# Before the MoE: other weights in a planner's choice of engines, batch 0's subtractions off GpSimd, its squares on TensorE, loads on SyncE alone

## The chip, the cores and the metric

The program runs on one core of one Trainium2 chip. A core has five engines with one in-order instruction queue each: PE (TensorE, matrix multiplies), DVE (VectorE), ACT (ScalarE), POOL (GpSimd) and SP (SyncE, which here only issues DMAs), beside 16 DMA engines. Engines wait for each other through semaphores. The metric is the device time of one execution in microseconds (us).

## The reference

Block-sparse attention, and after it a two-layer network on all tokens. Cut to what is computed:

```python
# q, k, v: (4 batches, 8 heads, 768 tokens, 64); sampled_blocks: (24, 3)
scores = (1 / sqrt(64)) * q @ k.T
mask = |block_i - block_j| <= 1, or block_i or block_j is the first or the last, or block_j is sampled for block_i   # blocks of 32
scores = where(mask, scores, -1e9)
attn = exp(scores - max(scores)); attn = attn / (sum(attn) + 1e-9)
x = (attn @ v) as 3072 tokens x 512
h = x @ w_in                                   # 512 x 2048
g = maximum(h, 0) + alpha * minimum(h, 0)
out = g @ w_out                                # 2048 x 512
```

Everything is float32 in memory.

## The kernel before

**Numbers.** A float32 operand is scaled by a power of two and split into two float16 parts: hi is the rounded value and lo the rest. A product is three float16 matmuls (hi*hi, hi*lo, lo*hi). `times` makes hi (one instruction: L385 on ACT, L387 on DVE, L389 on POOL). `rest` makes lo: one instruction on DVE (L393), two on POOL (L395 scales, L396 subtracts hi). The scale comes from a norm: ACT squares the tile and sums along a row (`squares`, L381), PE sums over the rows (`tot`, L471), and DVE turns the total into a power of two (`pow2`, L373 and L376).

**The weights** come as 16 tiles `wi` and 16 tiles `wo` of 512 KB. Their raw words lie in slots while three steps repack them: `emit_n1` (DVE, L840), `emit_n2` (ACT L845 or DVE L847), `emit_n3` (DVE, L852). Then a Gram matrix on PE (L861) and its row maxima on DVE (L867) give the norm; hi and lo follow, lo of `wi` and of the first half of `wo` through PE (`d`, L937 and L938) and an ACT copy (L942), lo of the second half of `wo` on DVE or POOL. Only when all 32 tiles have a scale is the factor `gsc` there, without which no MoE work starts.

**Attention.** The 3072 tokens are 12 chunks of 256, three to a batch. A chunk has 4 head pairs ("units"), a unit 4 steps of 128 query rows and one head; 192 steps in all. A step is: scores `sp` on PE (two steps at once, L586 and L592), bias and row minimum `e` on DVE (L602), exp on ACT (L609), the reciprocal of the row sum on DVE (`dn` L614, `rs` L615), P hi and P lo (`ph`), and a transposing DMA `pt` that SP issues (L630). Unit by unit PE multiplies P with v (`av`, L665); ACT and DVE split the result into `x` (L676, L681).

**MoE.** Eight times per chunk: `emit_up` on PE (`h`, L1034), `emit_act` on DVE (`g`, L1044 and L1045), `gh` on ACT (L1050), `gl` on POOL (L1055) and `emit_down` on PE (`o`, L1076). The MoE of a chunk is laid beside the attention of the next ones.

**What sets the order.** Nothing of it is written out by hand. Every piece of work is an operation of a planner (`Plan`) with a priority, costs for each engine that may do it, the operations it needs and the buffers it takes. `Plan.run` steps through a model of the engines: of the ready operations, in order of priority, each goes to the engine with the least waiting plus weight (`PREF`) times cost. The resulting list is the program's order on every engine, and it is kept: each queue runs in that order, whatever the chip does. `MAX4` are the costs of hi, `LOW4` those of lo, `LQ` those of issuing a load. `PL` gives by step whether P lo goes to POOL (g) or DVE (v); `LD`, and buffer counts in `BUFS`, limit how far weight loads run ahead; `V_WA` to `W_WB` are priorities of the weights against the attention steps.

Of the kernel before, what the change touches and what calls it, by code (L numbers as in the profile page):

```python
# [217 lines left out]
def attn_moe(ctx: ExitStack, tc: tile.TileContext, q, k, v, sampled, w_in, w_out, alpha, out):  # L218
# [391 lines left out]

    def emit_rs(n):
        T["rs", n] = new_small("rs")
        dn = new_small("dn")
        nc.vector.tensor_scalar(dn, T["su", n], 1e-9, 1.0 / PSCALE, ALU.add, ALU.mult)  # L614
# [8 lines left out]

    def emit_p_t(n):
        u, j = steps[n]
        w = chunks[units[u][0]][2]
        h, i = divmod(j, w)
        if ("pt", u, h) not in T:
            T["pt", u, h] = wt("pt", [P, 2 * NT, w * P], F16)
        nc.sync.dma_start_transpose(  # L630
            T["pt", u, h][:, :, i * P : (i + 1) * P], T["ph", n].rearrange("p a s -> p (a s)")
        )

    def emit_p_pe(n, x):
        u, j = steps[n]
        w = chunks[units[u][0]][2]
        h, i = divmod(j, w)
        if ("pt", u, h) not in T:
            T["pt", u, h] = wt("pt", [P, 2 * NT, w * P], F16)
        t = T["tp", n, x] = ps_o.tile([P, 2 * DM], F16, tag="o", name="tp")  # L640
        for g in range(NT):
            nc.tensor.transpose(t[:, g * P : (g + 1) * P], T["ph", n][:, x, g * P : (g + 1) * P], ident16)

    def emit_p_copy(e, n, x):
        u, j = steps[n]
        w = chunks[units[u][0]][2]
        h, i = divmod(j, w)
        dst = T["pt", u, h][:, x * NT : (x + 1) * NT, i * P : (i + 1) * P]
        src = T["tp", n, x][:, :S].rearrange("p (x j) -> p x j", j=P)
        if e == "ACT":  # L650
            nc.scalar.copy(dst, src)
        else:
            nc.vector.tensor_copy(dst, src)
# [103 lines left out]
    def attend(n):  # L757
# [18 lines left out]
        if n < P_PE:
            o_pt[n] = []
            for x, src in ((0, o_hi), (1, o)):
                tb = plan.buf("o")
                t = plan.op(n - 2, {"PE": 0.4}, lambda x=x: emit_p_pe(n, x), [src], [tb, ptbuf[u, h]], [pb])  # L780
                o_pt[n].append(plan.op(n - 2, {"ACT": 0.85, "DVE": 0.9}, lambda e, x=x: emit_p_copy(e, n, x), [t], [ptbuf[u, h]], [tb]))
            return
# [442 lines left out]
```

## Time and profile before

| what | value |
|---|---|
| runs | 838.78, 841.10 and 843.01 us, median 841.1 |
| the profiled execution: its own time, its span | 840.87 us, 839.1 us |
| PE, DVE, ACT, POOL busy | 94%, 77%, 60%, 65% of the span |
| mean granted TensorE clock | 0.981 |
| first `up` matmul of the MoE | 134.9 us |

The profile is one execution. "Busy" of PE is modelled, since matmuls are pipelined. The view by windows gives busy time per engine in each stretch; the view by line groups equal instructions with their mean; the chain of waits is followed back from the last instruction; each row of a timeline is a start, a duration and an instruction. A duration on DVE or POOL contains what the instruction was held up after it had been started.

### The profile page before, as it was taken

What the parts mean: (1) busy time and instruction counts of PE and PEld (TensorE: products, weight loads), DVE (VectorE), ACT (ScalarE), POOL (GpSimd) and SP (SyncE); (2) the same over time, 40 slices, a digit from 0 to 9 for tenths busy, and PEclk for the clock granted to TensorE, in tenths of its full rate; (3) what the DMA queues carried; (4) which work ended last, traced back from release to release, by engine and by line L of the source; (5) the groups of instructions that cost most, each with busy time, mean ns of one, the idle gap of its engine ahead of it and who ended that gap; (6) DMA issues with size and microseconds to landing.
All of it is one profiled execution on the core that took longest, in us unless ns stands there. A gap on an engine that the chain in (4) does not pass through costs nothing.

```text
span 839.1 us, 16792 instructions
## 1 busy us (share of the span) xinstructions
PE 787.2 (94%) x6255; PEld 497.9 (59%) x6255; DVE 648.7 (77%) x1403; ACT 506.6 (60%) x868; POOL 549.3 (65%) x442
## 2 busy tenths in 40 slices
PE   4767759999999999999999999999999999999997
PEld 2324326566666666666666666566656666666664
DVE  6889999979977679788788778788787787676222
ACT  7888778766747457756556467766474575454111
POOL 8556556967777577677766768558685777566221
PEclk9989988999999999999999999999999999999999
DMA  9999697979997788898989699978997688667100
GB/s 320 299 241 237 139 213 132 201 150 172 197 181 158 132 153 164 184 173 152 201 167 176 117 164 198 168 148 179 189 188 136 134 159 141 120 114 108 46 12 26
DMA packets 386449, 136.13 MB, mean 162 GB/s; under 512 B 350628, under 2 KB 379328, under 8 KB 386368
## 3 DMA queue, kind: packets, MB, share of 16 engines
q1 hardware_dynamic: 372704, 118.66, 75.5%
q10 hardware_dynamic: 13600, 16.39, 6.8%
q8 instruction: 49, 0.80, 0.4%
q14 instruction: 32, 0.26, 0.1%
q0 software_dynamic: 64, 0.02, 0.0%
HBM read 35.67 MB, written 6.29 MB: 50 GB/s over the span
## 4 chain that ended last, share of the span: by engine, by line
PE 79%; DVE 11%; issue 4%; DMA 3%; ACT 2%; POOL 2%; POOLq 0%; DVEq 0%; ACTq 0%
PE o L1076 28%; PE h L1034 27%; PE av L665 11%; PE sp L586 6%; PE sp L592 4%; DVE e L602 3%; DVE ph L393 2%; PE d L937 1%; DVE wo L852 1%; DVE wi L840 1%; DMA kf<-in_k_dram 1%; DMA pt<-ph 1%; DMA raw<-in_moe_w_out_dram 1%; POOL v L389 1%; DVE wi L852 1%
## 5 line engine op out<-in xcount | busy, mean ns | idle before, releaser
L1034 PE MATMUL h<-x,wi 128*128 128x256 f16 x2304 | 267.2, 273 | 0.0
L1034 PEld LDWEIGHTS <-wi 128*128 128x128 f16 x2304 | 220.5, 98 | 48.0 <-issue 15.2
L609 ACT ACTIVATE e<-e,nm 128x768 f32<-128x768 f32 x192 | 178.5, 930 | 92.1 <-DVE nm L602 85.7
L1076 PE MATMUL o<-wo,gh 128*128 128x512 f16 x768 | 229.1, 380 | 0.0
L602 DVE CUSTOM_DVE_ANT_0 e<-sp,bias,cs 128x768 f32<-128x768 f32 x192 | 188.3, 1011 | 21.3 <-PE sp L592 21.1
L396 POOL TENSOR_TENSOR ph<-e,ph 128x768 f16<-128x768 f32 x96 | 179.3, 1868 | 8.0
L1055 POOL TENSOR_TENSOR gl<-g,gh 128x512 f16<-128x512 f32 x96 | 119.3, 1245 | 99.3 <-ACT gh L1050 83.0
L1050 ACT CAST gh<-g 128x512 f16<-128x512 f32 x96 | 59.0, 616 | 152.3 <-DVE g L1045 149.4
L1076 PE MATMUL o<-wo,gl 128*128 128x512 f16 x384 | 145.5, 379 | 0.6 <-POOL gl L1055 0.6
L389 POOL TENSOR_SCALAR ph<-e,rs 128x768 f16<-128x768 f32 x70 | 76.5, 1094 | 104.1 <-ACT e L609 63.3
L393 DVE SCALAR_TENSOR_TENSOR ph<-e,rs,ph 128x768 f16<-128x768 f32 x96 | 123.5, 1288 | 6.8 <-ACT ph L385 4.0
L1044 DVE SCALAR_TENSOR_TENSOR g<-h,am 128x512 f32<-128x512 f32 x96 | 65.9, 687 | 77.0 <-PE h L1034 76.3
L385 ACT ACTIVATE ph<-e,rs 128x768 f16<-128x768 f32 x117 | 108.2, 930 | 24.1 <-ACT e L609 7.7
L1076 PEld LDWEIGHTS <-gh 128*128 128x128 f16 x768 | 69.1, 98 | 86.6 <-issue 15.9
L395 POOL TENSOR_SCALAR e<-e,rs 128x768 f32<-128x768 f32 x96 | 95.8, 998 | 34.4 <-ACT ph L385 30.5
L665 PE MATMUL av<-pt,v 128*64 128x256 f16 x1728 | 109.5, 283 | 6.7 <-DVE nm L602 6.3
L665 PEld LDWEIGHTS <-v 128*64 128x64 f16 x1728 | 95.2, 113 | 23.1 <-issue 15.2
L1045 DVE SCALAR_TENSOR_TENSOR g<-h,gsc,g 128x512 f32<-128x512 f32 x96 | 72.1, 751 | 3.4
L1076 PEld LDWEIGHTS <-gl 128*128 128x128 f16 x384 | 37.5, 98 | 46.3 <-POOL gl L1055 1.1
L586 PEld LDWEIGHTS <-qt 128*128 128x128 f16 x384 | 37.2, 99 | 46.2 <-issue 13.8
L586 PE MATMUL sp<-kt,qt 128*128 128x512 f16 x192 | 47.8, 331 | 8.3 <-DVE nm L602 7.8
L586 PE MATMUL sp<-ks,qt 128*128 128x512 f16 x192 | 47.9, 332 | 7.5 <-DVE nm L602 7.5
(144 smaller groups left out, 762.0 us busy)
## 6 DMA issues: line engine op xcount, KB each, us to landing
wo<-in_moe_w_in_dram SPq DMA_DIRECT2D x13, 512.0 KB, 8.2
ks<-kt SPq DMA_DIRECT2D x30, 192.0 KB, 3.6
raw<-in_moe_w_out_dram SPq DMA_DIRECT2D x11, 512.0 KB, 6.7
qf<-in_q_dram SPq DMA_DIRECT2D x7, 512.0 KB, 5.2
out_dram<-ob ACTq DMA_DIRECT2D x14, 256.0 KB, 3.8
vf<-in_v_dram SPq DMA_DIRECT2D x9, 384.0 KB, 6.4
kf<-in_k_dram SPq DMA_DIRECT2D x8, 384.0 KB, 4.2
kf<-in_k_dram ACTq DMA_DIRECT2D x8, 384.0 KB, 4.7
```

What stands on the lines that cost most here:

```text
L385: nc.scalar.activation(dst, src, AF.Copy, scale=scale)
L389: nc.gpsimd.tensor_scalar(dst, src, scale, 1.0, ALU.mult, ALU.mult)
L393: nc.vector.scalar_tensor_tensor(dst, src, scale, hi, ALU.mult, ALU.subtract)
L395: nc.gpsimd.tensor_scalar(tmp, src, scale, 1.0, ALU.mult, ALU.mult)
L396: nc.gpsimd.tensor_tensor(dst, tmp, hi, ALU.subtract)
L586: nc.tensor.matmul(T["sp", n + i][:, a:z], T["qt", u][:, h, i, :], (ks, kt)[i][:, h, a:z], start=True, stop=False)
L602: nc.vector.tensor_tensor_reduce(T["e", n], T["sp", n], bias[:, t0 + j % w, :], scale=T["cs", c][:, hp : hp + 1], scalar=3.0e38, op0=ALU.a ...
L609: nc.scalar.activation(T["e", n], T["e", n], AF.Exp, bias=T["nm", n], scale=-1.0, accum_out=T["su", n])
L665: nc.tensor.matmul(av[h * D : (h + 1) * D, : n * P], v2[:, h, t, vv, :], T["pt", u, h][:, pl * NT + t, :], start=(m == 0), stop=(m == len( ...
L1034: nc.tensor.matmul(ph[:, i, :], win(w, f, ct), x[:, ct, :], start=(m == 0), stop=(m == len(terms) - 1))
L1055: nc.gpsimd.tensor_tensor(T["gl", c, j], T["g", c, j], T["gh", c, j], ALU.subtract)
L1076: nc.tensor.matmul(T["o", c][t], g[:, i, t * P : (t + 1) * P], wout(w, f), start=(i == 0 and m == 0 and j in first_j), stop=(i == 1 and m ...
```

## The change

- The numbers that set priorities and weights differ, and until 130 us of the planner's clock (140 before) a second set `PREF0` holds. `SLOW`, a surcharge on POOL's and some of DVE's costs in that time, falls from 1.25 to 1.12.
- For the first 22 steps P lo goes by `PL0` ("ggv": two of three to POOL); before every second one did. A step from 22 on goes by `PL` as before.
- Batch 0: lo of k and v is DVE's alone (`LOW0`); lo of the second half of `wo` is DVE's alone as well.
- Batch 0: the norms of k and v come from Gram matrices on PE (6 matmuls a tile, 48 in all) and row maxima on DVE, not from ACT's squares.
- `dn` is an operation of its own that ACT may do.
- Loads and stores are issued by SP alone (`LQ` without ACT); 42 of them stood in ACT's queue.
- Six weight loads may be under way (4 before). The pools `wr` (2 raw slots) and `g` (4) become one pool `wr` of 4, which raw `wo` tiles, `g` and the output tiles share.
- Code that no step used (a transpose of P on PE) is gone.

```diff
-MOE_LAG = 10.618
+MOE_LAG = 10.973
-MOE_BOOST = 1.211
-V_WA = -18.766
-W_WA = 0.754
-V_WB = 1.134
-W_WB = 0.607
-LDP = 30.529
-PL_V = -33.326
-P_V = 0.73
+MOE_BOOST = 1.244
+V_WA = -11.421
+W_WA = 0.818
+V_WB = 2.562
+W_WB = 0.788
+LDP = 47.514
+PL_V = -45.149
+P_V = 2.094
 PL = "gv"
-LD = 4
-P_PE = 0
+NS0 = 22
+PL0 = "ggv"
+LD = 6
-PREF = {"PE": 1.0, "DVE": 1.896, "ACT": 1.009, "POOL": 0.778, "SP": 1.0}
-SLOW = 1.25
-UNTIL = 140.0
+PREF = {"PE": 1.0, "DVE": 1.928, "ACT": 1.347, "POOL": 1.033, "SP": 1.0}
+PREF0 = {"PE": 1.0, "DVE": 2.5, "ACT": 1.0, "POOL": 0.8, "SP": 1.0}
+SLOW = 1.12
+UNTIL = 130.0
-BUFS = {"wr": 2, ... "x": 2, "g": 4, ...}
+BUFS = {"wr": 4, ... "x": 2, ...}
...
+                    pref = PREF0 if now < UNTIL else PREF
+                    best = min(o.alts, key=lambda e: max(idle[e] - now, hold(o, e)) + load[e] + pref[e] * cost(o, e))
...
-    LQ = {"SP": 0.47, "ACT": 0.5}
-    MAX4 = {"DVE": (0.55, 0), "ACT": 0.85, "POOL": 1.08}
+    LQ = {"SP": 0.47}
+    MAX4 = {"DVE": (0.55, 0), "ACT": 0.88, "POOL": 0.95}
     LOW4 = {"DVE": (0.94, 0), "POOL": (1.1, 1.7)}
+    LOW0 = {"DVE": (0.94, 0)}
...
+    def emit_gram_kv(key, start, stop):
+        if start:
+            T["gkv", key[0]] = ps_h.tile([P, 512], F32, tag="h", name="gkv")
+        top = T[key].rearrange("p h e -> p (h e)").bitcast(BF16).rearrange("p (e w) -> p e w", w=2)[:, :, 1]
+        for i in range(NT):
+            m = top[:, i * P : (i + 1) * P]
+            nc.tensor.matmul(T["gkv", key[0]][:, :P], m, m, start=start and i == 0, stop=stop and i == NT - 1)
+
+    def emit_gram_kv_max(key, acc):
+        nc.vector.tensor_reduce(acc, T["gkv", key][:, :P], AX.X, ALU.max)
...
+    def emit_dn(e, n):
+        T["dn", n] = new_small("dn")
+        if e == "ACT":
+            nc.scalar.activation(T["dn", n], T["su", n], AF.Identity, bias=eps, scale=1.0 / PSCALE)
+        else:
+            nc.vector.tensor_scalar(T["dn", n], T["su", n], 1e-9, 1.0 / PSCALE, ALU.add, ALU.mult)
...
-        o = plan.op(prio, {"ACT": 0.85}, lambda: emit_k_sq(b, hp), [o], [], [fb])
+        if b == 0:
+            gb = plan.buf("h")
+            o = plan.op(prio, {"PE": 0.9}, lambda: emit_gram_kv(("kf", b, hp), True, True), [o], [gb], [fb])
+            o = plan.op(prio, {"DVE": 0.28}, lambda: emit_k_gmax(b, hp), [o], [], [gb])
+        else:
+            o = plan.op(prio, {"ACT": 0.85}, lambda: emit_k_sq(b, hp), [o], [], [fb])
...
-        o = plan.op(prio, LOW4, lambda e: emit_k_lo(e, b, hp), [o], [], [nb, fb])
+        o = plan.op(prio, LOW0 if b == 0 else LOW4, lambda e: emit_k_lo(e, b, hp), [o], [], [nb, fb])
...
-        o = plan.op(n - 2, {"DVE": 0.3}, lambda: emit_rs(n), [o])
+        o = plan.op(n - 2, {"DVE": 0.15, "ACT": 0.26}, lambda e: emit_dn(e, n), [o])
+        o = plan.op(n - 2, {"DVE": 0.15}, lambda: emit_rs(n), [o])
+        path = PL0[n % len(PL0)] if n < NS0 else PL[n % len(PL)]
...
-            o_wo[y] = plan.op(p - 3 + 0.1 * (y % HF), {"DVE": (0.67, 0), "POOL": (0.8, 1.25)}, lambda e, y=y: emit_w_lo(e, "wo", y), [o])
+            o_wo[y] = plan.op(p - 3 + 0.1 * (y % HF), {"DVE": (0.67, 0)}, lambda e, y=y: emit_w_lo(e, "wo", y), [o])
```

The order on the engines follows from all of this together. On POOL, behind the set-up of the masks and identities, stood hi and lo of three of batch 0's four k tiles (`kn`; L395 and L396 are the two halves of a lo), with the scaled identities `sid` and hi of weights (`wi`) between them:

```order
L389 TENSOR_SCALAR kn<-kf,ks 128x12x64
L395 TENSOR_SCALAR kf<-kf,ks 128x768
L396 TENSOR_TENSOR kn<-kf,kn 128x12x64
L926 TENSOR_SCALAR sid<-ident,ssc 128x128
L389 TENSOR_SCALAR wi<-wi,ssc 128x512
L395 TENSOR_SCALAR kf<-kf,ks 128x768
L396 TENSOR_TENSOR kn<-kf,kn 128x12x64
```

At the same place, in the changed program:

```order
L944 TENSOR_SCALAR sid<-ident,ssc 128x128
L394 TENSOR_SCALAR wi<-wi,ssc 128x512
L944 TENSOR_SCALAR sid<-ident,ssc 128x128
L394 TENSOR_SCALAR kn<-kf,ks 128x12x64
L394 TENSOR_SCALAR wi<-wi,ssc 128x512
L394 TENSOR_SCALAR kn<-kf,ks 128x12x64 x3
L944 TENSOR_SCALAR sid<-ident,ssc 128x128
L394 TENSOR_SCALAR wi<-wi,ssc 128x512 x2
```

The subtractions are gone, all four hi of k are there, and hi of weights is met more often.

On SP, the first loads before (`wo` is the place where raw `w_in` tiles wait, `raw` a slot for `w_out`; loads of `qf` and further `kf` stood in ACT's queue):

```order
L419 DMA kf<-in_k_dram 128x2x384
L419 DMA wo<-in_moe_w_in_dram 128x4x256 x3
L419 DMA kf<-in_k_dram 128x2x384
L419 DMA raw<-in_moe_w_out_dram 128x1024 x2
L419 DMA wo<-in_moe_w_in_dram 128x4x256
```

and now:

```order
L425 DMA wo<-in_moe_w_in_dram 128x4x256 x4
L425 DMA raw<-in_moe_w_out_dram 128x1024 x2
L425 DMA kf<-in_k_dram 128x2x384
L425 DMA qf<-in_q_dram 128x8x128
L425 DMA kf<-in_k_dram 128x2x384
L425 DMA raw<-in_moe_w_out_dram 128x1024
```

Six weight tiles stand ahead of the first k tile, and all of it is one queue.

On DVE, the stretch that ends with the fourth `x` (the last input of the first `up`), before:

```order
L887 TENSOR_TENSOR am_116<-al,gsc 128x16
L373 TENSOR_SCALAR uq<-ssq 128x1
L376 TENSOR_SCALAR sq<-uq 128x1
L1060 TENSOR_SCALAR fs_1458<-sv,s_wi 128x1
L1061 TENSOR_SCALAR fs_1458<-fs_1458,s_wo 128x1
L1062 RECIPROCAL fs<-fs_1458 128x1
L393 SCALAR_TENSOR_TENSOR wo<-wo,swo 128x512
L681 SCALAR_TENSOR_TENSOR x<-av,x 128x256
```

and now, with the rows behind it:

```order
L905 TENSOR_TENSOR am_118<-al,gsc 128x16
L398 SCALAR_TENSOR_TENSOR wo<-wo,swo 128x512
L690 SCALAR_TENSOR_TENSOR x<-av,x 128x256
L645 RECIPROCAL rs<-dn 128x1 x2
L1078 TENSOR_SCALAR fs_1522<-sv,s_wi 128x1
L1079 TENSOR_SCALAR fs_1522<-fs_1522,s_wo 128x1
```

The place is the same, and `gsc` and the fourth `x` still stand next to each other. The instruction that makes the fourth `x` is number 264 on DVE before and 251 now. On PE the same 96 score matmuls (24 steps) and 144 `av` matmuls stand ahead of the first `up` in both programs; the 48 matmuls of the Gram matrices are added.

More of the change, by code (lines that the diff above doesn't have):

```diff
@@ L257, in attn_moe @@
     nc.vector.memset(ones, 1.0)
+    eps = cpool.tile([P, 1], F32, name="eps")
+    nc.vector.memset(eps, 1e-9 / PSCALE)
     warm = cpool.tile([P, 1], F32, name="warm")
@@ L622, in emit_p_lo, with pt_tile @@
         rest(e, T["ph", n][:, 1, :], T["e", n], T["rs", n], T["ph", n][:, 0, :], T["e", n])
-    def emit_p_t(n):
[L625 to L653, printed above, removed]
+    def pt_tile(n):
+        u, j = steps[n]
+        h, i = divmod(j, 2)
+        if ("pt", u, h) not in T:
+            T["pt", u, h] = wt("pt", [P, 2 * NT, 2 * P], F16)
+        return T["pt", u, h][:, :, i * P : (i + 1) * P]
+    def emit_p_t(n):
+        nc.sync.dma_start_transpose(pt_tile(n), T["ph", n].rearrange("p a s -> p (a s)"))
     def emit_av(u):
@@ L769, in attend @@
         o = plan.op(n - 1, {"ACT": 0.94}, lambda: emit_exp(n), [o], [], [eb])
-        o = plan.op(n - 2, {"DVE": 0.3}, lambda: emit_rs(n), [o])
-        o = o_hi = plan.op(n - 1, MAX4, lambda e: emit_p_hi(e, n), [o], [pb], [eb])
-        lo = {"POOL": (1.1, 1.7)} if PL[n % len(PL)] == "g" else {"DVE": (0.94, 0)} if PL[n % len(PL)] == "v" else LOW4
-        o = plan.op(n - 1, lo, lambda e: emit_p_lo(e, n), [o], [], [pb, eb])
+        o = plan.op(n - 2, {"DVE": 0.15, "ACT": 0.26}, lambda e: emit_dn(e, n), [o])
+        o = plan.op(n - 2, {"DVE": 0.15}, lambda: emit_rs(n), [o])
         if i == 0:
             ptbuf[u, h] = plan.buf("pt")
[L776 to L782, printed above, removed]
+        path = PL0[n % len(PL0)] if n < NS0 else PL[n % len(PL)]
+        pb = plan.buf("ph")
+        o = plan.op(n - 1, MAX4, lambda e: emit_p_hi(e, n), [o], [pb], [eb])
+        lo = {"POOL": (1.1, 1.7)} if path == "g" else {"DVE": (0.94, 0)}
+        o = plan.op(n - 1, lo, lambda e: emit_p_lo(e, n), [o], [], [pb, eb])
         o_pt[n] = [plan.op(n - 1, {"SP": 1.7}, lambda: emit_p_t(n), [o], [ptbuf[u, h]], [pb], dma=2.2)]
@@ L979, in prep_wi @@
         for x in (f - 1, f):
-            o = plan.op(p + 0.1, {"ACT": 0.63, "DVE": (0.42, 0), "POOL": 0.9}, lambda e, x=x: emit_w_hi(e, "wi", x), [gs[-1], prev])
+            o = plan.op(p + 0.1, {"ACT": 0.63, "DVE": (0.42, 0), "POOL": 0.75}, lambda e, x=x: emit_w_hi(e, "wi", x), [gs[-1], prev])
             db = plan.buf("o")
@@ L1005, in prep_wo @@
         for y in range(x * HF, (x + 1) * HF):
-            o = plan.op(p - 3 + 0.1 * (y % HF), {"ACT": 0.63, "DVE": (0.42, 0), "POOL": 0.9}, lambda e, y=y: emit_w_hi(e, "wo", y), [o_swo[x], o_wo.get(y - 1)])
+            o = plan.op(p - 3 + 0.1 * (y % HF), {"ACT": 0.63, "DVE": (0.42, 0), "POOL": 0.75}, lambda e, y=y: emit_w_hi(e, "wo", y), [o_swo[x], o_wo.get(y - 1)])
             if WO_PE > x:
```

35 lines of the change are left out of this document (23 added, 12 removed).

## The prediction

> **What bounds the kernel now.** I read the page's parts 1 and 2 first.
>
> ```profile
> PE 787.2 (94%) x6255; PEld 497.9 (59%) x6255; DVE 648.7 (77%) x1403; ACT 506.6 (60%) x868; POOL 549.3 (65%) x442
> ...
> PE   4767759999999999999999999999999999999997
> ...
> DVE  6889999979977679788788778788787787676222
> ```
>
> The two digit rows tell two stages: up to the seventh slice (some 140 us) PE is half idle and DVE nearly full; after it PE is full to the end. The view by windows, cut where the first scores reach DVE (41.2), where the fourth `x` is made (133.2), and at 160, has the same in numbers (busy us per engine in the order PE, PEld, DVE, ACT, POOL, then granted clock and DMA):
>
> ```profile
> 0.00:20.00 20.00, 8.73 (x61) 4.73 (x61) 12.17 (x39) 14.08 (x22) 16.23 (x31) 1.00 0.96 316
> 20.00:41.20 21.20, 16.46 (x74) 7.22 (x74) 18.18 (x35) 17.52 (x27) 11.56 (x9) 0.92 1.13 304
> 41.20:133.20 92.00, 62.46 (x391) 32.45 (x390) 85.36 (x191) 73.74 (x116) 53.97 (x43) 0.86 0.98 205
> 133.20:160.00 26.80, 26.17 (x228) 17.20 (x227) 25.81 (x52) 20.68 (x37) 23.57 (x19) 0.98 0.76 154
> 160.00:839.10 679.10, 673.39 (x5509) 436.30 (x5506) 507.17 (x1089) 380.54 (x670) 444.02 (x342) 1.00 0.80 148
> ```
>
> From 133.2 on PE is the bound, and its work there is the same list of matmuls in both programs. So the end moves with the moment at which the fourth `x` and `gsc` are there; that is the quantity to forecast. Up to it DVE is busy 12.17 + 18.18 + 85.36 = 115.7 of 133.2 us. The chain of waits shows what came last (start, length, what):
>
> ```profile
> 116.90 1.73 POOL ph L396
> ...
> 121.05 7.61 DMA pt<-ph
> ...
> 128.70 4.06 PE av L665 x35
> ...
> 133.20 0.03 DVE x L681
> ```
>
> The last attention steps went through GpSimd, a slow `pt` transfer and `av`, while DVE finished the weights, and both met at 133.2. The forecast must therefore look at DVE's sum and at this path.
>
> **The change, part by part.** DVE first. Its groups up to 133.2 us, with count, busy and mean ns:
>
> ```profile
> L393 DVE SCALAR_TENSOR_TENSOR ph<-e,rs,ph 128x768 f16<-128x768 f32 x9 | 13.8, 1538 | 0.0
> L852 DVE SCALAR_TENSOR_TENSOR wi<-wo,wi 128x512 int32<-128x512 int32 x16 | 13.5, 851 | 0.3 <-ACT wo L845 0.2
> L852 DVE SCALAR_TENSOR_TENSOR wo<-raw,wo 128x512 int32<-128x512 int32 x16 | 13.2, 827 | 0.5 <-ACT raw L845 0.5
> L840 DVE TENSOR_SCALAR wi<-wo 128x512 int32<-128x512 int32 x16 | 12.9, 819 | 0.9 <-DMA wo<-in_moe_w_in_dram 0.9
> L840 DVE TENSOR_SCALAR wo<-raw 128x512 int32<-128x512 int32 x16 | 9.9, 627 | 0.4 <-DMA raw<-in_moe_w_out_dram 0.4
> L847 DVE SCALAR_TENSOR_TENSOR wo<-raw,wo 128x512 int32<-128x512 int32 x6 | 5.0, 832 | 0.0
> ...
> L614 DVE TENSOR_SCALAR dn<-su 128x1 f32<-128x1 f32 x20 | 2.9, 145 | 1.1 <-ACT e L609 0.9
> L847 DVE SCALAR_TENSOR_TENSOR wi<-wo,wi 128x512 int32<-128x512 int32 x4 | 2.7, 678 | 0.0
> L867 DVE TENSOR_REDUCE isum<-gram 128x1 bf16<-128x128 f32 x8 | 2.3, 286 | 2.4 <-PE gram L861 2.4
> L867 DVE TENSOR_REDUCE osum<-gram 128x1 bf16<-128x128 f32 x8 | 2.3, 284 | 1.4 <-PE gram L861 1.3
> L393 DVE SCALAR_TENSOR_TENSOR v<-vf,sv,v 128x768 f16<-128x768 f32 x2 | 1.9, 1012 | 0.0
> L387 DVE TENSOR_SCALAR wi<-wi,ssc 128x512 f16<-128x512 f32 x3 | 1.8, 599 | 0.0
> ```
>
> Held against their shortest (minimum, median, maximum ns, from the view by line), several of these means are long:
>
> ```profile
> L840 DVE TENSOR_SCALAR wi<-wo x16: 407/421/1862, 8.4 to 85.7; 128x512 int32<-128x512 int32 x16
> ...
> L852 DVE SCALAR_TENSOR_TENSOR wo<-raw,wo x16: 671/680/2130, 24.5 to 124.7; 128x512 int32<-128x512 int32 x16
> ...
> L393 DVE SCALAR_TENSOR_TENSOR ph<-e,rs,ph x9: 1004/1441/2412, 49.2 to 125.3; 128x768 f16<-128x768 f32 x9
> ...
> L393 DVE SCALAR_TENSOR_TENSOR kn<-kf,ks,kn x1: 1019/1019/1019, 6.6 to 6.6; 128x768 f16<-128x768 f32 x1
> ```
>
> Counted ahead of the fourth `x`, DVE loses five n2 (10 to 5), three P lo (9 to 6), six `dn` (20 to 14), one hi each of `kn`, `wi` and `wo`, and the copy of `kt`; it gains three `kn` lo (1 to 4), two v lo (2 to 4) and five row maxima. Instructions overlap by some 0.07 us, so I take the minimum less that: -5 x 0.61 - 3 x 0.93 - 6 x 0.15 - 1.4 - 0.5 + 5 x 0.95 + 5 x 0.2 = -2.9, and with the three `fs` and one scale that now stand behind the `x`, **-3.4 us**. At the means the same edits give about -5.7, but the means hold waiting that doesn't leave with the instruction. I take -3.4 and price the waiting by itself.
>
> That waiting is GpSimd's doing. A row of DVE's timeline and one of GpSimd's:
>
> ```profile
> 19.17 0.83 DVE L840 TENSOR_SCALAR wo<-raw 128x512 int32<-128x512 int32 x1
> ...
> 18.34 1.38 POOL L389 TENSOR_SCALAR wi<-wi,ssc 128x512 f16<-128x512 f32 x1
> ```
>
> A DVE operation that at its shortest needs 0.41 us takes 0.83 when it starts under a GpSimd instruction that ends at 19.72. Mean less minimum over the six groups of `ph`, L852, L840 and long L847 is 4.8 + 2.8 + 2.5 + 6.6 + 3.5 + 1.0 = 21 us up to 133.2. GpSimd was busy 16.23 + 11.56 + 53.97 = 81.8 us there, so each of its us costs DVE about a quarter. What GpSimd now has ahead of that point:
>
> ```profile
> L396 POOL TENSOR_TENSOR ph<-e,ph 128x768 f16<-128x768 f32 x10 | 17.9, 1788 | 0.8
> L395 POOL TENSOR_SCALAR e<-e,rs 128x768 f32<-128x768 f32 x10 | 11.3, 1128 | 8.2 <-ACT ph L385 8.0
> L389 POOL TENSOR_SCALAR ph<-e,rs 128x768 f16<-128x768 f32 x6 | 6.5, 1095 | 15.5 <-ACT e L609 8.9 <-DVE iu L373 5.9 <-ACT wo L942 0.8
> L389 POOL TENSOR_SCALAR wi<-wi,ssc 128x512 f16<-128x512 f32 x5 | 6.1, 1217 | 2.8 <-PE d L937 2.8
> ...
> L396 POOL TENSOR_TENSOR kn<-kf,kn 128x768 f16<-128x768 f32 x3 | 5.3, 1762 | 0.2
> L395 POOL TENSOR_SCALAR kf<-kf,ks 128x768 f32<-128x768 f32 x3 | 4.7, 1550 | 0.1
> L396 POOL TENSOR_TENSOR v<-vf,v 128x768 f16<-128x768 f32 x2 | 4.1, 2050 | 0.2
> ```
>
> Gone are the lo of three `kn` (-9.9) and two v (-6.4, with their scaling); new are four P lo (+11.7), four P hi (+4.4), four hi of `wi` (+4.9) and some 3 us of hi of `kn`, v and `wo` at some 1.1 each: +8 us. At a quarter that costs DVE **+2 us**, less 0.8 because a twentieth of the operations that can be held up is gone: +1.2. Its bounds are 0 and, if all eight us fall on DVE, +8. The Trainium skill's "SBUF — State Buffer", section "Who interferes with whom", says that whichever of the two starts first has their shared port for its whole instruction, against DVE operations with two SBUF inputs or in a two-port mode; the 0.83 us agrees. By that rule alone, with DVE exposed in half of its time, the 8 us would cost 4, and the edit on DVE's sum would come to nothing.
>
> For TensorE, a row of the chain near its start, and one of DVE's waits (total, times, longest):
>
> ```profile
> 26.95 0.87 PE gram L861 x8
> ...
> DVE x L681 <- ACT x L676: 1.6, 2, 1.3
> ```
>
> The 48 Gram matmuls cost PE 48 x 0.11 = 5 us back to back, in a stage where PE idles 133.2 - 87.7 = 45 us. They hide there; what can cost is a DVE queue that waits for them, as `isum` and `osum` waited 2.4 and 1.3 us. On ACT eight squares and 14 load issues leave, and five n2 and some `dn` arrive; it was busy 105 of 133 us, and DVE's rows above show 1.6 us of waiting for it. I put 0, with -2 to +4.
>
> SP's queue: six weight tiles now stand ahead of the first k tile. At the 316 GB/s of the first window 512 KB take 1.7 us, so k comes up to 10 us later; DVE spends that time on weight steps instead, one n1 and one n3 (1 us) per 1.7 us, and was itself busy only 12.17 of the first 20 us before. Stepping through the new order with these arrivals I come to the same 12 us of DVE work done at some 21 us. 0, with ±2. Behind the moved loads `kt` and `pt` transposes stand in the same queue; as the `v` loads need k's buffers, each waits for a `kn` lo on DVE, in the order in which DVE has them. The 7.61 us of the last `pt` had loads of ACT's queue beside it; in one queue the next q stands behind it, and `pt` may land sooner, but then DVE's weights are last. -0.7, from 0 to -2.
>
> After the fourth `x`: DVE has all eight lo of the second half of `wo` (each a P lo of 1.0 us on two thirds of its columns; four more than before), GpSimd none; PE idled 26.80 - 26.17 = 0.6 us there with DVE at 25.81. I put +0.5, between 0 and +3. Past 160 us DVE has 172 us to spare; 0. The tail is the same.
>
> Sum: -3.4 + 1.2 + 0.5 - 0.7 = **-2.4 us**. The profiled execution took 840.87 us, 0.2 under the median, so the forecast is 838.5 us.
>
> **The rivals.** *Waits go too (faster).* Past the start DVE waited for PE's Gram matrices (2.4 + 1.3), for the `av` behind `pt` (1.6), for exps and ACT's n2 (0.9 + 0.5) and a load (0.4): 7 us in all. More loads under way, a freer ACT and an earlier `pt` speak for it; that these waits come from the in-order queues, which still exist, against. Time: 840.87 - 2.4 - 5 to -7 = 832.5.
>
> *GpSimd becomes the bound (slower).* From 41.2 to 133.2 it worked 53.97 us and waited the rest, most of it for ACT's exp and P hi. Now 16 us come on top: 70 of 92, with two of three steps through 0.9 + 1.1 + 1.8 us in a row and four more `wi` hi between. If its waiting of 38 us shrinks only to 30, the sixteenth `ph` comes 8 us late, and `pt`, `av` and the first `up` with it: 849. It decides once these waits stay over some 22 us. For it: the last chain already ran through GpSimd. Against: before, its waits were for work that now comes no later.
>
> *It is all contention (no change).* If the eight us cost DVE 3 to 4, nothing is left: 841.
>
> **How the numbers follow.** 0.5% is about 4 us, what a measurement here can tell; faster means under 836.9, slower over 845.3. Main case 838.5 (835 to 842): 0.42, of which 0.10 lies under 836.9. Waits go: 0.27. Contention: 0.12. GpSimd or a blocked SP queue: 0.19. So faster 0.37, same 0.44, slower 0.19. The likeliest case alone has 835 to 842; with both signs the range is 829 to 848.
>
> **What would show it.** Right: the fourth `x` between 129 and 133 us, DVE's busy time up to it around 113, GpSimd's around 90, mean of L840 still near twice its minimum, PE full afterwards. Wrong: DVE idle by under 10 us before it (waits gone), or GpSimd over 75% from 41 us on with `av` waiting for `pt`; a first k tile whose norm keeps DVE idle near 15 us; PE under 26 of 27 us right after the first `up`.

## The result, and the profile after

The changed kernel took 834.96 us (median of 6 runs, 831.95 to 835.93); the kernel before, beside it, 841.98 (838.78 to 843.60). The ratio is 0.9915, 95% interval 0.9891 to 0.9939: faster by 0.85%, some 7 us. The forecast was 838.5 with 829 to 848, and "within 0.5%" the likeliest case; what came is the faster side, and, as the experiments show, for a reason that I had priced with the wrong sign.

The profiled execution took 835.07 us, with a span of 833.4. The view by windows, the columns as in the prediction (window, length, busy us of PE, PEld, DVE, ACT, POOL, then granted clock, DMA share, GB/s), cut where the first scores reach DVE and at the fourth `x`:

```profile
0.00:36.70 36.70, 22.07 (x152) 11.66 (x153) 27.38 (x73) 27.91 (x34) 18.02 (x34) 0.86 1.03 336
36.70:125.02 88.32, 63.18 (x419) 31.87 (x420) 80.17 (x177) 74.48 (x121) 69.61 (x57) 0.88 0.93 222
...
0.00:125.02 125.02, 85.24 (x570) 43.52 (x571) 107.56 (x250) 102.39 (x154) 87.62 (x90) 0.88 0.96 256
125.02:829.00 703.98, 700.62 (x5732) 454.14 (x5732) 556.52 (x1086) 381.46 (x744) 488.38 (x370) 1.00 0.69 147
```

The same cuts in the kernel before, as far as the prediction doesn't show them:

```profile
0.00:41.20 41.20, 25.19 (x134) 11.95 (x134) 30.35 (x72) 31.60 (x48) 27.79 (x39) 0.96 1.05 310
...
0.00:133.20 133.20, 87.64 (x522) 44.40 (x523) 115.71 (x263) 105.34 (x163) 81.75 (x82) 0.89 1.00 237
133.20:829.00 695.80, 694.07 (x5712) 451.39 (x5711) 530.79 (x1137) 399.91 (x704) 466.44 (x359) 1.00 0.80 149
```

The fourth `x` comes 8.2 us sooner (125.02 against 133.20): 4.5 us of it up to the first scores, 3.7 behind them. DVE's busy time up to it falls by 8.2 us too (115.71 to 107.56), and its idle time is the same, 17.5 us in both. GpSimd is busier by 5.9 us. So DVE did the stage in less busy time, beside a GpSimd that worked more.

DVE's groups up to the fourth `x`, with count, busy us and mean ns:

```profile
L870 DVE SCALAR_TENSOR_TENSOR wo<-raw,wo 128x512 int32<-128x512 int32 x16 | 12.8, 813 | 0.2 <-ACT raw L863 0.2
L870 DVE SCALAR_TENSOR_TENSOR wi<-wo,wi 128x512 int32<-128x512 int32 x16 | 12.3, 771 | 0.7 <-ACT wo L863 0.7
L858 DVE TENSOR_SCALAR wi<-wo 128x512 int32<-128x512 int32 x16 | 11.7, 734 | 5.0 <-DMA wo<-in_moe_w_in_dram 5.0
L858 DVE TENSOR_SCALAR wo<-raw 128x512 int32<-128x512 int32 x16 | 8.9, 567 | 0.0
L398 DVE SCALAR_TENSOR_TENSOR ph<-e,rs,ph 128x768 f16<-128x768 f32 x6 | 8.5, 1411 | 0.0
```

Where 16 instructions stand in both kernels, their means have fallen: L858 (L840 before) from 819 and 627 ns to 734 and 567, L870 on `wi` (L852) from 851 to 771. That is time in which they were held up.

At the fourth `x` itself, in the timeline:

```profile
125.02 0.41 DVE L690 SCALAR_TENSOR_TENSOR x<-av,x 128x256 f16<-128x256 f32 x1
...
125.49 0.55 PE L611 MATMUL sp<-kt,qt 128*128 128x512 f16 x2 [2.61 <-DVE x L690]
```

PE had stood 2.6 us for it. From here to the end of the span the changed kernel takes 708.4 us, the one before 705.9: 2.5 us of the 8.2 are given back.

### The profile page after: what moved, and what is told of

The parts are those of the page before. It is cut to its first block, busy times and chain, and to the rows that moved or that the text cites. A ratio compares the mean times of both kernels' runs of the same rounds, so it can differ in the third digit from the quotient of the medians.

```text
span 833.4 us, 16815 instructions
## 1 busy us (share of the span) xinstructions
PE 786.3 (94%) x6303; PEld 497.7 (60%) x6303; DVE 664.8 (80%) x1336; ACT 483.9 (58%) x898; POOL 576.0 (69%) x460
## 5 line engine op out<-in xcount | busy, mean ns | idle before, releaser
L394 POOL TENSOR_SCALAR ph<-e,rs 128x768 f16<-128x768 f32 x95 | 97.9, 1031 | 144.5 <-PE sp L617 33.5
L401 POOL TENSOR_TENSOR ph<-e,ph 128x768 f16<-128x768 f32 x100 | 188.2, 1882 | 8.3
L1073 POOL TENSOR_TENSOR gl<-g,gh 128x512 f16<-128x512 f32 x96 | 125.3, 1307 | 57.4 <-ACT gh L1068 36.7
L398 DVE SCALAR_TENSOR_TENSOR ph<-e,rs,ph 128x768 f16<-128x768 f32 x92 | 135.6, 1474 | 4.3 <-ACT ph L390 2.8
L400 POOL TENSOR_SCALAR e<-e,rs 128x768 f32<-128x768 f32 x100 | 112.2, 1122 | 10.7 <-ACT ph L390 7.8
L674 PE MATMUL av<-pt,v 128*64 128x256 f16 x1728 | 105.4, 277 | 5.4 <-DVE nm L627 5.2
L674 PEld LDWEIGHTS <-v 128*64 128x64 f16 x1728 | 92.1, 111 | 22.4 <-issue 15.2
L390 ACT ACTIVATE ph<-e,rs 128x768 f16<-128x768 f32 x75 | 69.4, 930 | 22.7 <-DVE rs L645 18.7
L611 PEld LDWEIGHTS <-qt 128*128 128x128 f16 x384 | 37.6, 99 | 35.3 <-issue 13.2
L611 PE MATMUL sp<-kt,qt 128*128 128x512 f16 x192 | 48.2, 334 | 5.8 <-DVE x L690 4.1
```

The source lines that it names most:

```text
L394: nc.gpsimd.tensor_scalar(dst, src, scale, 1.0, ALU.mult, ALU.mult)
L398: nc.vector.scalar_tensor_tensor(dst, src, scale, hi, ALU.mult, ALU.subtract)
L400: nc.gpsimd.tensor_scalar(tmp, src, scale, 1.0, ALU.mult, ALU.mult)
L401: nc.gpsimd.tensor_tensor(dst, tmp, hi, ALU.subtract)
L611: nc.tensor.matmul(T["sp", n + i][:, a:z], T["qt", u][:, h, i, :], (ks, kt)[i][:, h, a:z], start=True, stop=False)
L674: nc.tensor.matmul(av[h * D : (h + 1) * D, : n * P], v2[:, h, t, vv, :], T["pt", u, h][:, pl * NT + t, :], start=(m == 0), stop=(m == len( ...
```

## The experiments

The table holds one profiled execution of each kernel, worked out from the instructions of its trace. Up to the fourth `x`, **list** is the sum over DVE's instructions of the shortest duration that the same form has in any of these traces; **held** is what their durations add to it; **idle** is the time of the fourth `x` less DVE's busy time. (List and held together exceed busy time by some 15 us, since neighbours overlap.) Two columns give GpSimd's time in subtractions (TENSOR_TENSOR) and in one-input work (TENSOR_SCALAR); spans on GpSimd are rough. "Behind" is the span behind the fourth `x`. The ratio is to the kernel before in the same session.

| kernel | ratio, 95% interval | fourth x | list | held | idle | GpSimd subtr. | GpSimd one-input | behind |
|---|---|---|---|---|---|---|---|---|
| before | 1 | 133.2 | 102.6 | 28.1 | 17.5 | 27.3 | 47.1 | 705.9 |
| changed | 0.9915, 0.9891 to 0.9939 | 125.0 | 98.9 | 23.8 | 17.5 | 24.3 | 56.3 | 708.4 |
| more subtractions | 1.0049, 1.0032 to 1.0066 | 134.1 | 98.9 | 33.3 | 17.2 | 37.2 | 56.8 | 708.6 |
| more one-input work | 0.9991, 0.9980 to 1.0003 | 131.6 | 98.9 | 29.0 | 19.0 | 24.5 | 69.4 | 708.0 |
| half of P lo to DVE | 0.9889, 0.9868 to 0.9909 | 122.0 | 105.9 | 16.9 | 14.9 | 11.7 | 48.2 | 707.5 |
| all P lo to DVE | 0.9925, 0.9906 to 0.9945 | 126.5 | 112.9 | 13.2 | 16.6 | 0 | 39.4 | 707.5 |
| k, v subtractions undone | 0.9950, 0.9933 to 0.9968 | 129.6 | 93.9 | 28.6 | 21.5 | 33.3 | 61.3 | 707.4 |
| before, k, v subtr. on DVE | 1.0001, 0.9985 to 1.0017 | 132.9 | 107.5 | 20.7 | 19.8 | 18.1 | 40.3 | 705.5 |
| squares on ACT again | 0.9948, 0.9930 to 0.9967 | 126.8 | 97.8 | 21.7 | 22.0 | 24.0 | 57.0 | 706.8 |
| loads by ACT too | 0.9974, 0.9961 to 0.9987 | 130.0 | 98.9 | 26.8 | 19.9 | 24.0 | 55.1 | 707.0 |
| changed, one due time | 1.0067, 1.0048 to 1.0086 | 129.9 | 97.8 | 22.8 | 24.1 | 24.7 | 56.1 | 713.4 |
| changed, old numbers | 1.0112, 1.0090 to 1.0134 | 138.7 | 107.1 | 18.5 | 28.4 | 24.4 | 37.8 | 711.7 |
| changed, old preferences | 1.0232, 1.0210 to 1.0255 | 129.0 | 99.8 | 22.3 | 21.7 | 24.6 | 44.7 | 729.4 |
| before, new numbers | 1.0448, 1.0418 to 1.0479 | 134.4 | 99.0 | 28.4 | 21.4 | 33.3 | 53.9 | 742.1 |

The first two rows are the case: list -3.6, held -4.3 (before rounding), idle 0. Held can be split by what GpSimd was doing when the DVE instruction started. Under subtractions it is 13.8 us before and 8.9 after, under one-input work 12.1 and 12.6, under other GpSimd instructions 0.2 and 0.8, and with GpSimd idle 2.0 and 1.5. So held fell under the subtractions, though GpSimd's time in them fell by only 3.0 us, and it hardly rose under 9.2 us more of one-input work.

### Does GpSimd's work set DVE's time?

My theory after the traces was contention, against the rival that only DVE's shorter list counts. Two kernels give GpSimd more work before the MoE and leave DVE's list alone. The second writes the same values again:

```diff
     def emit_p_lo(e, n):
         rest(e, T["ph", n][:, 1, :], T["e", n], T["rs", n], T["ph", n][:, 0, :], T["e", n])
+        if e == "POOL" and n < NS0:
+            n_lo[0] += 1
+            if n_lo[0] % 2 == 1:
+                nc.gpsimd.tensor_tensor(T["ph", n][:, 1, :], T["e", n], T["ph", n][:, 0, :], ALU.subtract)
```

> The changed kernel with eight of GpSimd's subtractions for P lo before the MoE done twice (the second writes the same values again): +8 two-input instructions of 1.75 us, 14 us more of GpSimd, which was busy 87.6 of 125 us. No instruction of DVE changes. Theory A (two-input instructions of GpSimd hold DVE up): DVE's busy time up to the fourth x grows by 14 x 0.4 to 0.65 = 5.5 to 9 us, and the time to 840 to 844 us. Theory B (contention is small, own work decides): DVE's busy time grows by under 2 us; GpSimd has room, so 835 to 837 us.

Its window up to the fourth `x`:

```profile
0.00:134.12 134.12, 89.83 (x570) 45.69 (x571) 116.94 (x250) 103.40 (x154) 100.61 (x97) 0.83 0.89 238
```

A group of GpSimd's there (L657 is the added line) and one of DVE's, with count, busy us, mean ns:

```profile
L657 POOL TENSOR_TENSOR ph<-e,ph 128x768 f16<-128x768 f32 x7 | 13.3, 1904 | 0.5
...
L875 DVE SCALAR_TENSOR_TENSOR wo<-raw,wo 128x512 int32<-128x512 int32 x16 | 15.7, 990 | 0.2 <-ACT raw L868 0.2
```

DVE has the same 250 instructions and is busy for 116.94 us instead of 107.56; the 16 `wo` steps take 990 ns on average instead of 813. Held rises by 9.5 us for 12.9 us more of subtractions, 0.73 us per us, and 9.0 of the 9.5 lie in DVE instructions that started during a subtraction; the fourth `x` comes 9.1 us later; the time was 845.17 us. DVE's idle time doesn't grow (17.2), so the added work acted on DVE's durations, not by a late `pt`. The rival falls.

The other kernel adds about as much time in one-input instructions:

```diff
     def emit_p_lo(e, n):
+        if e == "POOL" and n < NS0:
+            nc.gpsimd.tensor_scalar(T["e", n], T["e", n], 1.0, 1.0, ALU.mult, ALU.mult)
         rest(e, T["ph", n][:, 1, :], T["e", n], T["rs", n], T["ph", n][:, 0, :], T["e", n])
```

> The changed kernel with a multiplication by 1.0 on GpSimd (TENSOR_SCALAR, 128x768, in place) ahead of every P lo that GpSimd makes before the MoE: +15 one-input instructions of some 1.1 us, 16 us more of GpSimd, about as much as in the run with more subtractions. Theory A with a difference between kinds (one-input instructions hold DVE up little: 6.6 us in 56 us of them by overlap): DVE +2 us, 836 to 838 us. Theory A without it (each busy us of GpSimd costs the same, a quarter): +4 us, 839 to 841 us, like the other run. Theory B: 835 to 836 us.

Its window, and the added group (L654):

```profile
0.00:131.59 131.59, 88.89 (x570) 45.30 (x571) 112.56 (x250) 102.32 (x153) 98.63 (x104) 0.84 0.90 240
```

```profile
L654 POOL TENSOR_SCALAR e<-e 128x768 f32<-128x768 f32 x14 | 16.0, 1143 | 2.8 <-ACT ph L391 2.4
```

Held rises by 5.2 us for 13.1 us more of one-input work, 0.39 per us, about half the price of subtractions; in DVE instructions that started during one-input work it rises from 12.6 to 18.5 us. The time was 841.56 us, just over what I had put for equal prices (839 to 841), since 1.6 us of idle time came on top. Both kinds cost, and work added here costs more per us than the quarter of the forecast.

Then the other way, taking P lo off GpSimd (first every second one, then all of the first 22 steps):

```diff
     def emit_p_lo(e, n):
+        e = "DVE" if n < NS0 and n % 2 == 1 else e
```

> The changed kernel with every second P lo of the first 22 steps back on DVE (some 7 of the 15 that GpSimd has now leave it: -12 us of two-input and -6.4 us of one-input instructions), all else in the same order. Contention by the prices of the two runs with more GpSimd work: -12 x 0.73 - 6.4 x 0.36 = -11 us on DVE's durations against +7 x 0.95 = +6.7 us of its own: net -4, some 831 us. If the price falls as GpSimd empties (all that lies under two-input instructions in the changed kernel is 8.7 us): -5 + 6.7 = +2, 837 us. Own work alone: +6.7, 842 us.

```diff
     def emit_p_lo(e, n):
+        e = "DVE" if n < NS0 else e
```

> The changed kernel with all P lo of the first 22 steps on DVE (15 leave GpSimd: -25 us of two-input, -14 us of one-input instructions), so that GpSimd has no two-input instruction there. DVE gets 15 x 0.95 = +14 us of its own. Contention: the 8.7 us under two-input instructions vanish and a third of the rest: -12 us, net +2, 837 us. Linear prices would give -25 x 0.73 - 14 x 0.36 = -23, more than all there is (17.9), so at most -18: 831 us. Own work alone: 849 us. This run also tells whether a one-input instruction alone holds DVE up: then L858's mean stays over its shortest 0.41 us.

The window of the first, then the window of the second, and of the second the view by line (minimum, median, maximum ns):

```profile
0.00:122.00 122.00, 87.00 (x570) 44.88 (x571) 107.12 (x257) 100.49 (x152) 66.61 (x76) 0.86 0.97 259
```

```profile
0.00:126.51 126.51, 89.61 (x570) 46.66 (x571) 109.89 (x264) 101.34 (x152) 47.27 (x62) 0.87 0.95 250
```

```profile
L859 DVE TENSOR_SCALAR wi<-wo x16: 409/419/1009, 4.7 to 84.6; 128x512 int32<-128x512 int32 x16
L859 DVE TENSOR_SCALAR wo<-raw x16: 398/412/424, 11.9 to 113.8; 128x512 int32<-128x512 int32 x16
```

Seven P lo more on DVE lengthen its list by 7.0 us and shorten what it is held by 6.9: its busy time stays (107.12), 2.6 us of idle time go, and the fourth `x` comes 3.0 us sooner. The 831 us of the expectation came, but by another sum: linear prices had asked for 11 us less held. 831.57 us was the fastest time of all and beats the kernel before by 1.1%. Against the changed kernel the ratios, 0.9889 and 0.9915, have intervals that overlap; that it beats this one too is shown by the fourth `x` of one trace each, not by the times.

All P lo on DVE gives up 10.6 us of held time for 14.0 of list: 835.12 us, no gain. The first 20.7 us taken off GpSimd were worth 6.9 us, the next 20.5 us 3.7: the price falls as GpSimd empties.

### The parts of the change, one at a time

The five subtractions of k and v, undone in the changed kernel, and done alone in the kernel before:

```diff
     def emit_k_lo(e, b, hp):
+        e = "POOL" if b == 0 and hp > 0 else e
...
     def emit_v_lo(e, b, hp):
+        e = "POOL" if b == 0 and hp > 1 else e
```

```diff
     def emit_k_lo(e, b, hp):
+        e = "DVE" if b == 0 else e
...
     def emit_v_lo(e, b, hp):
+        e = "DVE" if b == 0 else e
```

> The changed kernel (fourth x at 125.0 us, 835 us) with one thing undone: the five subtractions of the first batch (lo of three k pairs and of two v pairs) go back from DVE to GpSimd, scaling included, everything else in the order of the changed kernel. Theory A, contention: DVE is held up by GpSimd's two-input instructions (in the kernel before, 17.7 us of DVE's 25.5 us over its shortest durations lay under them, 27.2 us of GpSimd). Then DVE loses 5 x 0.95 = 4.8 us of its own, but GpSimd gains 16 us, 9.5 of them subtractions, and these cost DVE 9.5 x 0.65 = 6 us: fourth x at 125 to 131 us, 836 to 841 us. Theory B, own work: the gain came from DVE's shorter list alone; then this kernel is faster still, fourth x at some 120.5 us, 831 us.

> The kernel before (fourth x at 133.2 us, 842 us) with one part of the change alone: the five subtractions of the first batch that GpSimd made (three k pairs, two v pairs) on DVE, all else in the order of the kernel before. The runs with more GpSimd work priced it: 12.9 us more of two-input instructions made DVE's durations 9.4 us longer (0.73 per us), 14.1 us more of one-input ones 5.1 us (0.36 per us). Contention by these prices: DVE +4.8 us of its own, GpSimd -9.5 us of two-input (-6.9) and -6.5 us of one-input work (-2.3): net -4.4, some 838 us; by the undoing of the same step in the changed kernel (fourth x 4.6 us later, time 2.5 us longer) -2.5 to -4.6: 837 to 839.5 us. Own work alone: +4.8, 847 us. If it stays at 842, the step gives nothing by itself and the gain lies in the new order as a whole.

The windows of the undone one, then of the other, cut at the first scores:

```profile
0.00:39.20 39.20, 22.30 (x159) 11.73 (x160) 29.27 (x70) 28.77 (x34) 25.64 (x39) 0.91 1.00 333
39.20:129.59 90.39, 66.23 (x411) 33.59 (x411) 78.85 (x176) 73.36 (x119) 75.54 (x62) 0.82 0.87 205
```

```profile
0.00:42.45 42.45, 24.74 (x134) 11.77 (x134) 29.30 (x75) 32.94 (x48) 17.02 (x33) 0.96 1.05 313
42.45:132.89 90.44, 61.60 (x391) 30.57 (x390) 83.80 (x194) 72.97 (x116) 48.89 (x39) 0.87 0.94 203
```

In the kernel before, moving them shortens held by 7.4 us and lengthens the list by 5.0, as contention has it, but DVE then waits 2.3 us longer, and the time stays (ratio 1.0001), where I had expected 837 to 839.5 us of contention. Undone in the changed kernel, they lengthen held by 4.8, shorten the list by 5.0, and make DVE wait 4.0 us longer; the fourth `x` comes 4.6 us later and the time was 837.50 us. So in the changed order the step brings DVE's busy time about as much as it costs, and in the old one it saves some 2.5 us, which DVE then waits. What it is worth at the end hangs on the waits around it.

The norms of batch 0 back on ACT:

```diff
-            o = plan.op(prio, {"PE": 0.9}, lambda: emit_gram_kv(("kf", b, hp), True, True), [o], [gb], [fb])
-            o = plan.op(prio, {"DVE": 0.28}, lambda: emit_k_gmax(b, hp), [o], [], [gb])
+            o = plan.op(prio, {"PE": 0.9}, lambda: emit_k_sq(b, hp), [o], [gb], [fb])
+            o = plan.op(prio, {"DVE": 0.28}, lambda: None, [o], [], [gb])
...
```

> The changed kernel with the sums of squares of the first batch's k and v undone: eight squares on ACT (8 x 1.03 us) in place of 48 Gram matmuls on TensorE and five row maxima on DVE; the norm is then the one of the kernel before. Everything else keeps its order. If TensorE's 5 us hide and ACT has room, as I forecast (a term of 0): DVE loses 5 x 0.2 us and some waiting for the Gram matrices, ACT goes from 102 to 110 of 125 us, 833.5 to 836 us. Rival: the relief of ACT is where the gain came from (exps and n2 came sooner): then fourth x goes from 125.0 to 129 or later and the time to 839 or more.

One of DVE's waits (total, times, longest), and the window:

```profile
DVE ku L378 <- PE tot L477: 3.0, 3, 1.3
```

```profile
0.00:126.79 126.79, 91.41 (x522) 45.39 (x523) 104.84 (x247) 107.65 (x169) 87.69 (x90) 0.87 0.93 249
```

DVE's list and held time both fall (by 1.2 and 2.1 us), but its idle time rises by 4.5 us, 3.0 of it where it waits for norms (`ku`); the fourth `x` is 1.8 us later and the time 837.68 us. The fourth `x` says 1.8 us for this part, the ratios 2.8 with 2.5 either way; less than the rival asked for (129 us or later, 839 or more).

The loads, every third of the first 43 issued by ACT (14 loads; the transfers that copy `kt` to `ks` stay with SP):

```diff
     def load(e, dst, src):
-        (nc.sync if e == "SP" else nc.scalar).dma_start(dst, src)
+        n_load[0] += 1
+        (nc.scalar if n_load[0] < 44 and n_load[0] % 3 == 0 else nc.sync).dma_start(dst, src)
```

> The changed kernel with every third of its first 43 loads issued by ACT instead of SP, in the same order of the program (14 loads; the kernel before had 14 there). My forecast of this step was 0 with 2 us to either side, and 0.7 us for a pt that lands sooner in one queue. If that stands: 834 to 837 us. If the one queue is where the gain came from: fourth x at 128 us or later, 838 us or more. If the one queue costs (DVE waits 5.0 us for input weights, 3.7 of them at once, near the start): fourth x 2 to 4 us sooner, 831 to 833 us.

The start of DVE's timeline in this kernel, then in the changed one:

```profile
4.71 0.99 DVE L861 TENSOR_SCALAR wi<-wo 128x512 int32<-128x512 int32 x1 [3.65 <-DMA wo<-in_moe_w_in_dram]
9.83 0.43 DVE L861 TENSOR_SCALAR wi<-wo 128x512 int32<-128x512 int32 x1 [4.12 <-DMA wo<-in_moe_w_in_dram]
```

```profile
4.78 0.93 DVE L858 TENSOR_SCALAR wi<-wo 128x512 int32<-128x512 int32 x1 [3.71 <-DMA wo<-in_moe_w_in_dram]
6.23 0.43 DVE L858 TENSOR_SCALAR wi<-wo 128x512 int32<-128x512 int32 x1 [0.52 <-DMA wo<-in_moe_w_in_dram]
```

The second weight tile comes 3.6 us later when part of the loads goes through ACT's queue; the first scores reach DVE at 40.9 us instead of 36.7, and the fourth `x` at 130.0. By the ratios (0.9974 and 0.9915) that costs 0.6%, 5 us, with about half of that as the uncertainty. One queue is worth several us in this order, outside my 0 with 2 to either side. This is a split of my own, not the one of the kernel before, whose order had its k tile first.

`dn` on ACT, lo of `wo` on DVE alone, the six weight loads under way, the shared pool and a `pt` that lands sooner were not tried by themselves.

### Or is it the order?

Undone in the changed kernel, these three parts put the fourth `x` off by 2 to 5 us each; done alone in the old one, the one that I tried gave nothing. That is what one would see if the planner's numbers had been fitted to this code, so that most departures from this order make it worse. Four kernels test that; in each the planner makes a new order. First the changed code with the old numbers, and the old code with the new ones (`PL0`, `NS0`, `LD` and the buffer counts stay with their code):

```diff
-V_WA = -11.421      # changed kernel, and likewise the others of these numbers,
+V_WA = -18.766      # PREF, SLOW, UNTIL, MAX4; PREF0 = PREF
...
```

> The changed kernel's code (Gram matrices for k and v, subtractions on DVE, loads by SP, shared buffers) with the numbers of the choice among engines as they were before (due times, weights, one set of preferences for the whole run), so the order is planned anew and P lo goes to GpSimd less often. If the structure of the code carries the gain: 833 to 837 us. If the numbers, that is the order that came of them, carry it: 840 us or more. Between them it is shared. DVE's durations and what lies over their shortest, up to the fourth x, tell which.

> The kernel before (842 us) with the changed kernel's numbers (due times, weights, the preferences for the first 130 us and for after), its code as it was: squares on ACT, subtractions shared with GpSimd, loads by SP and ACT. The changed code with the old numbers took 850.9 us, so the numbers are worth 16 us there. If they are better by themselves: 830 to 838 us here. If they only fit the code that they came with: 842 us or more, fourth x at 133 us or later, with DVE idle for longer than the 17.5 us before it.

Window and largest waits of DVE in the first:

```profile
0.00:138.69 138.69, 91.62 (x570) 49.38 (x571) 110.33 (x262) 107.71 (x170) 68.17 (x76) 0.82 0.83 228
```

```profile
DVE kss L488 <- PE gkv L485: 4.1, 1, 4.1
DVE x L690 <- ACT x L685: 4.1, 3, 1.8
DVE dn L641 <- ACT e L634: 2.8, 4, 1.1
```

The changed code with the old numbers takes 850.85 us, 1.1% more than the kernel before. Its held time is the third lowest of all (18.5), but DVE idles for 28.4 us, among others behind the new Gram matrices (`gkv`), the wait that my prediction had named as the thing that can cost. The old code with the new numbers takes 878.33 us: the numbers are no better by themselves either. There the loss lies behind the fourth `x`, in waits of PE:

```profile
PE sp L588 <- DVE x L683: 10.1, 5, 3.7
PE sp L588 <- DVE nm L604: 4.5, 5, 2.1
PE av L667 <- DVE nm L604: 4.3, 3, 1.9
```

Then only the preferences among engines put back:

```diff
-PREF0 = {"PE": 1.0, "DVE": 2.5, "ACT": 1.0, "POOL": 0.8, "SP": 1.0}
+PREF0 = PREF        # and PREF, SLOW, UNTIL, MAX4 as before
```

> The changed kernel with the old preferences among engines (one set for the whole run, as before, with the old costs of the hi pieces and the old point of switching), but with its own due times. With all old numbers it took 850.9 us, fourth x at 138.7 us, DVE idle for 28.4 us before it against 17.5. If the choice among engines carries the difference: 845 us or more, the same long waits. If the due times carry it (what is started when): 834 to 840 us, idle near 17 us.

860.86 us; the fourth `x` comes at 129.0, and the rest is again lost behind it (729.4 us to the end against 708.4). The preferences matter as much as the first of my two alternatives said, but not through the long waits ahead of the fourth `x` that it named.

Last, one due time moved slightly:

```diff
-V_WA = -11.421
+V_WA = -11.0
```

> The changed kernel with one number of its due times moved slightly (the first due time of the weights from -11.42 to -11.00): no edit of the work, but the order is planned anew and differs from there on, on every engine. If a gain of some us stands for a step of the change: 833.5 to 836.5 us. If every new order is a draw of its own, by where waits and GpSimd's work happen to fall: 838 us or more, or 832 or less, with DVE's time over its shortest durations and its idle time both moved by some us.

Its window, and DVE's largest waits:

```profile
0.00:129.93 129.93, 91.35 (x570) 48.58 (x571) 105.81 (x244) 104.17 (x160) 88.36 (x89) 0.86 0.91 245
```

```profile
DVE iu L378 <- PE gram L888: 5.3, 4, 2.6
DVE wi L858 <- DMA wo<-in_moe_w_in_dram: 5.2, 4, 3.9
DVE vtot L488 <- PE gkv L485: 2.6, 1, 2.6
```

847.08 us. From the same code, DVE's list and held time come out even lower (97.8 and 22.8), but it waits 24.1 us in place of 17.5 (the wait for `wi` loads, 5.2 us here, stands in the changed kernel too, with 5.0), and 5 more us are lost behind the fourth `x`. A step of 0.4 in one number costs 12 us by the medians, more than the whole change gained. So a new order does shift the time by more than any single part of this change, through waits; how wide such orders scatter in general, one neighbour can't tell.

## Why the prediction was right, and where it was wrong

**The bound.** Right for this pair: with DVE nearly full up to the fourth `x` and PE behind it, the end moved with it. In all ten kernels that keep one of the two orders but for the piece that is moved or added, 705.5 to 708.6 us lie behind the fourth `x`. As a rule it was too broad: where the order was planned anew it was 711.7 to 742.1.

**DVE's own work, -3.4 us.** The list is 3.6 us shorter. Counting edits at their shortest durations, and pricing the waiting by itself, was the step that held best.

**Contention, +1.2 us: the step that failed.** It measured -4.3. I had taken one price, a quarter, for each of GpSimd's us and applied it to the net 8 us more. GpSimd is indeed busier, by 5.9 (87.6 us, "around 90" was said), yet DVE is held up less. The five subtractions that left with their scaling were worth 7.4 us of held time for 15.9 us of GpSimd, 0.46 per us, by the run that does this step alone. Between that run and the changed kernel GpSimd gains 22.2 us and held rises by 3.1, 0.14 per us; this difference holds all the rest of the change, so it is a remainder and no measurement of one thing. The net of the two can't be had from an average. From the forecast to the result, -2.9 to -8.2 at the fourth `x`, are 5.3 us, and this term's miss is 5.5. (List and held give -7.9. The 0.7 us that I had put on a sooner `pt` don't show: DVE's idle time is the same.) What failed is counting GpSimd's us instead of looking at which instruction meets which: held fell by 4.9 us under subtractions and rose by 0.5 under one-input work. A row of DVE's timeline and one of GpSimd's in the changed kernel:

```profile
80.13 1.88 DVE L858 TENSOR_SCALAR wi<-wo 128x512 int32<-128x512 int32 x1
```

```profile
79.66 2.06 POOL L401 TENSOR_TENSOR ph<-e,ph 128x768 f16<-128x768 f32 x1
```

An instruction of 0.41 us that starts 0.5 us into a subtraction ends 0.3 us after it; all DVE instructions that started with GpSimd idle were held for 1.5 us together. By the Trainium skill's rule, page "SBUF — State Buffer", section "Who interferes with whom", the sum would by the prediction's estimate have come to 841; that the second of the two to start is blocked to the other's end, these rows bear out.

**The Gram matrices, 0 (-2 to +4).** In the changed order they bring 1.8 us at the fourth `x`, within the bounds; in the order by the old numbers DVE waited 4.1 us for one of them.

**SP's queue, 0 with 2 to either side.** Too narrow: with a third of its first 43 loads on ACT the changed kernel's fourth `x` comes 5.0 us later. As walked, the weight steps came first (the second at 6.23 us), and DVE's idle time up to the first scores fell from 10.9 to 9.3 us; that was part of why the first scores came 4.5 us sooner, the rest was held time (7.3 us before, 4.4 after, summed to that point).

**After the fourth `x`, +0.5 (0 to +3).** It was 2.5 us, within the bounds: from the fourth `x` to its last matmul PE was busy for 701.0 us in place of 699.6, and idle for 3.4 in place of 2.3.

**The rivals.** "Waits go too" has the time (832.5), not the mechanism: DVE idles 17.5 us in both; its waits only changed their places, with 5.0 us for weight loads now and 4.5 us for the norm of a k tile before. Of the 0.37 for a faster time 0.27 rested on this rival, so as far as the prediction foresaw a faster time, it was partly lucky. "GpSimd becomes the bound": it was busy 69.6 of 88.3 us from the first scores on, 79%, over the mark that I had set, but PE's `av` waited for scores of DVE, not for `pt`:

```profile
PE av L674 <- DVE nm L627: 5.2, 2, 4.5
```

(The last `pt` to land before the longer of these two waits ended, at 106.88 us, had come at 105.56.) DVE itself waited 0.7 us for GpSimd in all. So GpSimd was not the bound; it cost through DVE's durations. "All contention" had the right mechanism and the wrong sign.

**The signs.** The fourth `x` fell outside 129 to 133 us, DVE's busy time was 107.6, not 113; PE had 26.3 of the 26.8 us behind it, as said:

```profile
125.00:151.80 26.80, 26.31 (x221) 17.72 (x221) 25.06 (x50) 18.89 (x34) 22.21 (x16) 0.94 0.47 106
```

What the prediction lacked altogether is the order as a cause by itself. It priced the steps and left the planner's new order at 0, and the runs show orders of the same work 12 us apart. The 7 us are what this code with these numbers gives; they aren't the sum of steps that would give it elsewhere.

## What to carry to other kernels

When two engines hold each other up, don't price work that moves between them at the average: separate the shortest durations of the list from what lies over them, and expect the latter to change with every new order. Where a planner sets the order, time a neighbour of its numbers before crediting any step; and a step that wins busy time on the full engine may only turn it into a wait, as the subtractions did in the old order.
